# Removing DRAM row copies and following the array's current shape in a two-branch training step

## The chip, the cores and the metric

The kernel runs on one core of one Trainium2 chip. The time is the device time of one execution in microseconds (us), lower is better.

## The reference

The program computes a layer's output and all its gradients. The input `x` (2048 tokens of 512) is normalised to `xn`, and the output is `x + A(xn) + B(xn)`. All large arrays are bf16.

Branch A is attention with a memory that is carried along: the tokens are cut into 64 segments of 32, and each segment attends, with 32 heads of 128, to 8 memory rows and itself. The memory rows' own results are the memory of the next segment:

```python
mem = mem0
for s in range(n_seg):
    xs = x[:, s * seg_len:(s + 1) * seg_len, :].copy()
    h = jnp.concatenate([mem, xs], axis=1)
    q = jnp.einsum('btd,dhe->bhte', h, Wq)
    k = jnp.einsum('btd,dhe->bhte', h, Wk)
    v = jnp.einsum('btd,dhe->bhte', h, Wv)
    scores = jnp.einsum('bhqe,bhke->bhqk', q, k) * scale
    scores = jnp.where(mask[None, None], scores, -1000000000.0)
    p = _softmax(scores, axis=-1)
    o = jnp.einsum('bhqk,bhke->bhqe', p, v)
    o = jnp.einsum('bhte,hed->btd', o, Wo)
    mem = o[:, :M, :].copy()
    outs.append(o[:, M:, :])
```

Branch B is an MLP (512 to 1792 to 512) with a squared ReLU. `reference` returns the output and the gradients of `x`, `mem0`, the four attention weights and the MLP's weights and biases, by `jax.vjp`.

## The kernel before

The work goes in four stages. **First** the normalisation and the MLP, forward and backward, in 8 groups of 256 tokens (to about 245 us). It stores the MLP's activations and their gradients (`S_AT`, `S_GT1`). **Forward** come the 64 segments, one after the other, since each needs the memory of the one before: `chain(s)`. **Backward** the same 64 steps run from the last to the first. **Last** come the attention's weight gradients, 16 groups of long 128x128 products with 512 columns, at L1690 and L1694.

A block is four segments, 128 tokens. In the projections, a segment's 32 rows (8 memory rows in place of the first 8 tokens, and 24 tokens) are the narrow weights of 128x32 products: four such products lie side by side in the array, one for each group `j` of heads. The first 8 tokens of every segment need not wait in this chain: their projections do not depend on the memory, and their attention is not needed by the next segment. They are handled four segments at a time, off the chain: these are the "lead" rows of `l_proj`, `l_qkv`, `l_attn` (forward), `l_pre` and `l_post` (backward), whose tiles end in L (`ps_qL`, `ps_scL`, `ps_gL`).

TensorE's array thus takes three shapes, which the code calls by a letter: "f" is 128x128, "w" is 128x32 (four column groups), "d" is 32x32 on the diagonal. Projections, scores and memory products are "w", transposes (`to_T` at L546, `transpose_to` at L427) are "f", attention-weighted sums (`diag`) are "d".

Off-chain work fills the waits of the chain. In the forward stage these are the lead rows and the MLP's weight gradients, `dw_unit`: 14 units, each with 16 chunks of 128 tokens; a chunk is loaded into one of five buffers `sx` and enters two 128x128 products with 512 columns into `ps_dw` (L1254). Units 7 to 13 also transpose their result (`ps_wT`).

Nothing here runs in the order of the source. Every operation is handed to a planner, `_Plan` (L109), with its costs, its shape and what it reads and writes. `run` (L166) then fixes the order of all instructions of all engines: it ranks an operation by the longest path behind it, plus a hand-tuned number from the tables `BIAS`, and takes next what can start first. `PAR` has three constants for each stage: `grace`, added to the start of off-chain work, `idle`, how long an engine may be kept waiting for a better operation, and `keep`, a penalty on an operation whose shape differs from the array's. The planner counts 0.105 us for a change of shape (`_TURN`).

The results that the backward stage and the weight gradients need go through DRAM. Some are stored and then copied from DRAM to DRAM into another order of rows: `S_V` and `S_K` (keys and values of each segment), whose first 8 rows of each head group go on to `S_VM` and `S_KM`; the lead rows of `S_XN` and of the output gradient, to `S_HNL` and `S_GOL`; those of `S_B`, to `S_BL`; the lead rows of the output, which go to `S_OL` and from there to `out_0`. At a block's end, `blk_out` transposes all 128 rows of its input, memory rows included, back (`ps_hN`, backward `ps_gN`) and stores them to `S_HNA` and `S_GOA` by four DMAs. `HNc` and `GOc` are loaded from these for the weight gradients. All these DMAs but a few go through SyncE's queue (SP), in order.

Of the kernel before, what the change touches and what calls it, by code (L numbers as in the profile page):

```python
# [10 lines left out]
PAR = ((0.3, 0.3, 0.0), (0.61, 7.94, 4.04), (0.09, 2.05, 17.32))  # L11
BIAS_0 = None
BIAS_1 = {
    "l_proj": (
        47.2, 6.5, -41.1, 1.2, 0.8, -33.9, -14.2, 11.4, 20.3, -5.1, -5.3, -14.4, 17.4, 1.5, 7, 20.1, 4.7,
        25.3, -22.2, 55.6, -37, 19.3, -97.5, -1.4, 23, -6.1, -29.3, 48.8, 4.1, 4.5, 52.1, -159.3,
    ),
    "blk_in": (
        11.4, -35.6,
    ),  # L20
# [4 lines left out]
    ),  # L25
    "chain": (
# [4 lines left out]
    ),  # L31
    "blk_out": (
        16.8, -102.8, -36.2, -171.6, -10.2, -72.7, -50.6, -74.7, -96.5, 48.6,
    ),
    "l_attn": (
# [16 lines left out]
    ),  # L52
    "l_pre": (
        46.2, 1.1, -8.1, -100.3, 71, -115.1, -66.8, -4.6, 0.3, -83.5, 0.5, -9.3, -80.7, -12.7, -35.4, -15.9,
        26.3, 9.2, -131.2, 6, 10.9, -47, -9.6, -40.9, 6.9, -128.5, -6.9, -9.4, -61.5, 28.5, -31.2, -38.8,
        -146.2,
    ),
    "load": (
        -43.9, 14.3, -32.2, 2.7, 17.6, -33.7, -80.9, -102.8, 27.2, -48.1, 12.4, -79.8, 33.3, -39.3, -48,
        -45.5, -93.3, -170.2, -64.2, -40.6, -31.9, -8.7, -42, -6.3, 6.8, 15.9, 1.3, 13.8, -17.6, -62.2,  # L60
    ),
    "chain": (
# [5 lines left out]
    ),  # L68
    "blk_out": (
        -22.4, 26.1, -106.9, -65.1, -53.3, 31.4, -76.5,  # L70
    ),
    "l_post": (
# [3 lines left out]
    ),  # L76
# [12 lines left out]
_LINE = 128  # L89
_FETCH = 4.2  # L90


class _PE(dict):
    shape = None
    n = 8


def pe(cost, shape, n=8):
    x = _PE(PE=cost)
    x.shape = shape  # L100
    x.n = n
    return x
# [206 lines left out]
def kernel(  # L309
# [59 lines left out]
    JQ = 4  # L369
# [1373 lines left out]
```

## Time and profile before

| | |
|---|---|
| median of 3 runs | 2802.92 us (2802.28 to 2803.98) |
| span of the profiled execution, first to last instruction | 2798.3 us |
| mean granted TensorE clock | 0.995 |

The page gives no other time for the profiled execution than its span; the runs' median is 4.6 us longer than this span. TensorE's share of time is in two rows: PE is the products, PEld the loads of their weights, which overlap with them.

Rows of a timeline have the start, the length, engine, line and operation, then out<-in by the program's names, the array's shape (128\*32), the moving operand (128x512) and how many were merged. Products are pipelined: the next one starts well before the recorded end of the one before.

### The profile page before, as it was taken

The numbers are of one execution on the slowest core, as the hardware profiler recorded it, in microseconds if no ns is written. First come the engines' busy times: TensorE is split into PE (matmuls) and PEld (weight loads), VectorE is DVE, ScalarE is ACT, GpSimd is POOL, SyncE is SP. The second block draws the span as 40 slices with busy tenths as digits, with TensorE's granted clock in tenths as the row PEclk, the third lists the DMA queues.
The fourth block names the chain that finished last, engine by engine and source line by source line (L and its number), as shares of the span: only waits on it lengthen the run. The fifth ranks groups of instructions, "written<-read, shape, count | busy, mean of one in ns | idle before, by whom it ended". The sixth has DMA issues, their size and how long they took to land.

```text
span 2798.3 us, 125071 instructions
## 1 busy us (share of the span) xinstructions
PE 2664.6 (95%) x54888; PEld 1538.5 (55%) x55072; DVE 1327.3 (47%) x3327; ACT 985.8 (35%) x2012; POOL 824.8 (29%) x2431
## 2 busy tenths in 40 slices
PE   8998999999999999999999999999999899999999
PEld 6664555555555555575555555555555444444444
DVE  5544455555455555565455455555455402232322
ACT  4333444444444444364444444444444300000000
POOL 1111111111111111145555555555555301112210
PEclk9999999999999999999999999999999999999999
DMA  6657656555557566647777676777766698788861
GB/s 211 202 172 205 180 160 175 164 166 163 156 169 186 169 185 175 177 118 178 187 181 187 179 189 179 189 192 190 188 182 177 201 344 273 232 255 270 257 185 42
DMA packets 499792, 530.91 MB, mean 190 GB/s; under 512 B 223845, under 2 KB 325398, under 8 KB 497070
## 3 DMA queue, kind: packets, MB, share of 16 engines
q1 hardware_dynamic: 480254, 463.06, 59.9%
q0 software_dynamic: 15056, 53.56, 5.6%
q8 instruction: 430, 7.05, 1.1%
q10 hardware_dynamic: 3936, 6.29, 0.7%
q14 instruction: 116, 0.95, 0.1%
HBM read 249.77 MB, written 237.52 MB: 174 GB/s over the span
## 4 chain that ended last, share of the span: by engine, by line
PE 45%; DVE 4%; issue 3%; DMA 3%; ACT 1%; POOL 1%; SPq 0%; DVEq 0%; ACTq 0%; POOLq 0%
PE ps_gw L1690 14%; PE ps_dRA L1370 8%; PE ps_gw L1694 5%; PE ps_gO L538 3%; PE ps_dRL L1370 3%; PE ps_d L624 2%; DMA dLN<-S_GNL 2%; PE ps_d L573 1%; PE ps_d L599 1%; PE ps_gOT L429 1%; PE ps_d L588 1%; PE ps_gm L1524 1%; PE ps_gL L538 1%; PE ps_dL L1481 1%; PE ps_dP L1468 1%
## 5 line engine op out<-in xcount | busy, mean ns | idle before, releaser
L1370 PE MATMUL ps_dRA<-WA,dT 128*32 128x512 bf16 x6144 | 377.0, 381 | 5.3 <-issue 2.5
L1690 PE MATMUL ps_gw<-WA,WB 128*128 128x512 bf16 x1505 | 330.6, 379 | 1.6
L1690 PEld LDWEIGHTS <-WB 128*128 128x128 bf16 x1896 | 185.4, 98 | 225.0 <-issue 1.7
L538 PEld LDWEIGHTS <-PA 128*32 128x32 bf16 x8192 | 195.4, 96 | 192.3 <-DVE PA L1190 22.3
L435 ACT CAST dN<-ps_d 128x512 bf16<-128x512 f32 x372 | 207.4, 590 | 184.7 <-PE ps_d L599 112.3
L1370 PEld LDWEIGHTS <-dT 128*32 128x32 bf16 x6144 | 151.8, 96 | 154.2 <-DVE dT L517 17.3
L433 DVE CAST gwo<-ps_gw 128x512 bf16<-128x512 f32 x64 | 40.0, 685 | 399.9 <-PE ps_gw L1690 268.5
L435 ACT CAST gwo<-ps_gw 128x512 bf16<-128x512 f32 x64 | 33.1, 598 | 510.2 <-PE ps_gw L1690 357.3
L517 DVE STREAM_TRANSPOSE dT<-dN 128x256 f32<-128x256 f32 x384 | 165.4, 437 | 72.1 <-ACT dN L435 66.5
L1020 POOL TENSOR_TENSOR P<-P,rsA 128x320 bf16<-128x320 bf16 x64 | 46.2, 722 | 458.8 <-DVE rsA L1015 244.1
L624 PEld LDWEIGHTS <-PB 32*32 32x32 bf16 x8192 | 119.8, 92 | 76.4 <-DVE PB L1168 23.9
L1701 POOL DMA_DIRECT2D out_dram<-gwo x96 | 71.6, 753 | 293.9 <-ACT gwo L435 265.1
L538 PE MATMUL ps_q<-WA,PA 128*32 128x512 bf16 x2048 | 145.2, 382 | 5.5 <-DVE PA L1190 3.7
L1039 PE MATMUL ps_RA<-WB,OT 128*32 128x256 bf16 x4096 | 129.0, 277 | 17.7 <-DVE OT L517 13.6
L538 PE MATMUL ps_k<-WA,PA 128*32 128x512 bf16 x2048 | 144.9, 381 | 0.3 <-DVE PA L1190 0.3
L435 ACT CAST kN<-ps_k 128x512 bf16<-128x512 f32 x125 | 73.4, 587 | 194.1 <-PE ps_k L538 172.2
L538 PE MATMUL ps_v<-WA,PA 128*32 128x512 bf16 x2048 | 140.7, 379 | 0.0
L1039 PEld LDWEIGHTS <-OT 128*32 128x32 bf16 x4096 | 103.9, 98 | 46.2 <-DVE OT L517 32.0
L538 PE MATMUL ps_gO<-WB,PA 128*32 128x512 bf16 x2048 | 126.4, 380 | 1.0 <-DVE PA L1528 1.0
L611 POOL COPY BDL<-bPLL 32x64 bf16<-32x64 bf16 x256 | 60.4, 236 | 218.4 <-PE ps_d L573 210.4
L433 DVE CAST qN<-ps_q 128x512 bf16<-128x512 f32 x62 | 42.9, 692 | 171.5 <-PE ps_q L538 169.5
L1254 PE MATMUL ps_dw<-sx,anT 128*128 128x512 bf16 x339 | 108.2, 384 | 6.6 <-DMA sx<-S_XN 2.8
(315 smaller groups left out, 5300.8 us busy)
## 6 DMA issues: line engine op xcount, KB each, us to landing
S_GN<-dN SPq DMA_DIRECT2D x192, 256.0 KB
WA<-S_GN SPq DMA_DIRECT2D x150, 256.0 KB
S_Q<-qN SPq DMA_DIRECT2D x64, 256.0 KB
S_K<-kN SPq DMA_DIRECT2D x64, 256.0 KB
S_V<-vN SPq DMA_DIRECT2D x64, 256.0 KB
S_ON<-oN SPq DMA_DIRECT2D x64, 256.0 KB
bqN<-S_Q SPq DMA_DIRECT2D x64, 256.0 KB
bkN<-S_K SPq DMA_DIRECT2D x64, 256.0 KB
```

The costliest lines, as they stand in the source:

```text
L433: nc.vector.tensor_copy(out, in_)
L435: nc.scalar.copy(out, in_)
L517: self.plan.add({"DVE": 0.445}, lambda e, half=half: nc.vector.transpose(words(dst, half).rearrange("p (i c r) -> p i c r", i=4, c=2), src ...
L538: nc.tensor.matmul(bk()[32 * j:32 * (j + 1), :], lhsT=win(dc), rhs=Wt(dc, c0), start=(dc == 0), stop=(dc == DC - 1), tile_position=(0, 32 ...
L611: f(q_(dst, j)[:, :, j, 0:c], q_(src_f(), j))
L624: nc.tensor.matmul(bk()[32 * j:32 * j + m, k * P:(k + 1) * P], lhsT=lf(j, i), rhs=rf(j, i), start=(k == 0 and x == 0), stop=(x == n - 1), ...
L1039: nc.tensor.matmul(bk()[32 * c:32 * (c + 1), :], lhsT=sg.rows(OTt, i, j), rhs=Wo[:, JQ * i + j, dh * DH:(dh + 1) * DH], start=(i == 0 and ...
L1254: nc.tensor.matmul(bks[x]()[:], lhsT=anT[x][:, c, :], rhs=sx[z][:], start=(c == 0), stop=(c == TC - 1))
L1370: nc.tensor.matmul(bk()[32 * j:32 * (j + 1), :], lhsT=sg.rows(XT, i, j), rhs=wtf(t, i, j), start=(first and i == 0), stop=(last and i == N ...
L1690: nc.tensor.matmul(bks[n](), lhsT=HNc[:, rc, dc * P:(dc + 1) * P], rhs=gns[y][:, hf * 512:(hf + 1) * 512], start=(y == 0), stop=(y == NRC ...
L1694: nc.tensor.matmul(bks[n](), lhsT=gns[y][:, k * P:(k + 1) * P], rhs=GOc[:, rc, :], start=(y == 0), stop=(y == NRC - 1))
L1701: nc.gpsimd.dma_start(outWs[t][dc * P:(dc + 1) * P, 4 * hf:4 * hf + 4, j, :], wt[:].rearrange("p (i e) -> p i e", i=4))
```

## The change

**DRAM layouts.** `S_K`, `S_V`, `S_VL`, `S_ON`, `S_ONL`, `S_GN` and `S_GNL` get another order of dimensions, so that the memory rows of a block, or the rows of a weight gradient's chunk, can be read by one strided DMA. `S_VM`, `S_KM`, `S_HNA`, `S_HNL`, `S_GOA`, `S_GOL`, `S_BL` and `S_OL` go, with their copies. `blk_out` packs only the 8 memory rows of each segment (GpSimd), turns them by four 32-column products and stores them with one DMA to `S_HM` (backward `S_GM`). `HNc` and `GOc` are put together from `S_XN` (the output gradient for `GOc`) and these, by more and smaller loads. The rows of `VR` and `VTL` come in another order, so the GpSimd copies into `VT` read with a stride.

**Shapes.** An off-chain product can be given as "wf": the planner lets it run in the array's shape of the moment, "w" or "f", and changes the shape for it only if the array has neither. This holds for `ps_dw`, `ps_wT` and the lead rows' transposes (`ps_qLT`, `ps_kLT`, `ps_gLT`). As "w", a 128x128 product is four 128x32 products.

**Pairs.** `dw_unit` loads two chunks with one DMA, into three buffers of two chunks.

**Fewer products.** The lead scores `ps_scL` and their gradient `ps_dPL` take one product with 64 columns where there were two with 32. The chain's mask product covers 256 columns, not 320.

The planner's constants `PAR` of the forward and backward stages and all tables `BIAS` of these are new.

```diff
-PAR = ((0.3, 0.3, 0.0), (0.61, 7.94, 4.04), (0.09, 2.05, 17.32))
+PAR = ((0.3, 0.3, 0.0), (0.37, 216.29, 18.84), (0.09, 14.67, 24.36))
...
-                turn = o.shape not in (None, shape)
+                turn = bool(o.shape) and shape not in o.shape
...
-    S_K = dt_([NSEG, P, HW], BF16, "S_K")
-    S_V = dt_([NSEG, P, HW], BF16, "S_V")
+    S_K = dt_([TC, RA, JQ, SPB, HW], BF16, "S_K")
+    S_V = dt_([TC, RA, JQ, SPB, HW], BF16, "S_V")
...
+    def mixed_rows(t, c0, c1, base, mems):
+        ops = []
+        for v in range(SPB):
+            ops.append((t[RA * v + M:RA * (v + 1), c0:c1, :], base[c0 * P:c1 * P].rearrange("(c v r) d -> v r c d", v=SPB, r=RA)[v, M:]))
+        for v in range(SPB):
+            ops.append((t[RA * v:RA * v + M, c0:c1, :].rearrange("k c (y z) -> k (c y) z", y=DC),
+                        mems[c0:c1, :, M * v:M * (v + 1), :].rearrange("c y k z -> k (c y) z")))
+        return ops
...
     def transpose_to(ps_ap, in_ap, base=0, form="f"):
+        if form == "w":
+            for c in range(4):
+                x = slice(32 * c, 32 * c + 32)
+                nc.tensor.transpose(ps_ap[x], in_ap[:, x], ident[:], tile_position=(0, 32 * c))
+            return
...
         def to_T(self, kind, nm, src, skeys, out_f, okeys, prio):
+            form = "wf" if prio else "f"
...
-                    for c in range(2):
-                        for j in range(JQ):
-                            nc.tensor.matmul(q_(ps, j)[:, i, 32 * c:32 * c + 32], lhsT=qLT[p][:, i, j, :],
-                                             rhs=KT[p][:, :, i * JQ + j, M * c:M * c + M],
+                    for j in range(JQ):
+                        nc.tensor.matmul(q_(ps, j)[:, i, :].rearrange("p (c v k) -> p v c k", c=2, k=M), lhsT=qLT[p][:, i, j, :],
+                                         rhs=KT[p][:, :, i * JQ + j, 0:2 * M].rearrange("p v (c k) -> p v c k", c=2),
...
-                nc.tensor.matmul(q_(bs_(), j).rearrange("p i k -> p (i k)"), lhsT=ident[:, 32 * j:32 * (j + 1)],
-                                 rhs=maskA[:].rearrange("p i k -> p (i k)"), start=True, stop=False,
+                nc.tensor.matmul(q_(bs_(), j)[:, :, M:KA], lhsT=ident[:, 32 * j:32 * (j + 1)],
+                                 rhs=maskA[:, :, M:KA], start=True, stop=False,
...
-            for nm, D_, S_ in (("S_V", S_VM, S_V), ("S_K", S_KM, S_K)):
-                sg.dma(lambda D_=D_: mrow(D_[b])[:, M * v:M * (v + 1), :], lambda S_=S_: mrow(S_[s])[:, 0:M, :],
-                       [(nm, s)], [(nm + "M", b, v)])
...
-        sx = [tl("sx%d" % x, [P, D]) for x in range(5)]
+        sx = [tl("sx%d" % x, [P, 2, D]) for x in range(3)]
...
                 def mm(e, c=c, z=z):
+                    w = 32 if e == "w" else P
                     for x in range(2):
-                        nc.tensor.matmul(bks[x]()[:], lhsT=anT[x][:, c, :], rhs=sx[z][:], start=(c == 0), stop=(c == TC - 1))
-                A(pe(0.435, "f", 2), mm, [("sx", z), ("anT", 0, c // HC), ("anT", 1, c // HC)], [bks[0], bks[1]])
+                        for m in range(0, P, w):
+                            nc.tensor.matmul(bks[x]()[m:m + w, :], lhsT=anT[x][:, c, m:m + w], rhs=sx[z][:, c % 2, :], start=(c == 0),
+                                             stop=(c == TC - 1), tile_position=(0, m))
+                A(pe(0.435, "wf", 2), mm, [("sx", z), ("anT", 0, c // HC), ("anT", 1, c // HC)], [bks[0], bks[1]])
...
         def blk_out(b):
-            bk = sg.bank("f", [P, D], BF16, "ps_gN")
+            A({"POOL": 0.3}, lambda e: nc.gpsimd.tensor_copy(
+                gNat[:, 0:P].rearrange("p (c v k) -> p c v k", c=DC, k=M), gT[p].rearrange("p c (v r) -> p c v r", r=RA)[:, :, :, 0:M]),
+              [("gT", p)] + [("gm", p, v) for v in range(SPB)], ["gNat"])
+            bk = sg.bank("f", [P, P], F32, "ps_gN")
...
             def tr(e):
                 for dc in range(DC):
-                    transpose_to(bk()[:, dc * P:(dc + 1) * P], gT[p][:, dc, :])
+                    nc.tensor.matmul(bk()[32 * dc:32 * (dc + 1), :], lhsT=gNat[:, 32 * dc:32 * (dc + 1)], rhs=ident[:],
+                                     start=True, stop=True, tile_position=(0, 32 * dc), skip_group_check=True)
```

More of the change, by code (lines that the diff above doesn't have):

```diff
@@ L100, in pe @@
     x.shape = shape
-    x.n = n
+    x.n = {k: n * (4 if k == "w" and len(shape) > 1 else 1) for k in shape}
     return x
@@ L176, in run @@
         free, loose, used = {}, {}, {}
-        shape = None
+        shape = "-"
         line = count = 0
@@ L285, in run @@
                     elig.append(u)
-            seq.append((o, e))
+            seq.append((o, form if form and len(o.shape) > 1 else e))
         assert len(seq) == len(ops)
@@ L383 @@
     S_XN = dt_([S, D], BF16, "S_XN")
-    S_HNA = dt_([S, D], BF16, "S_HNA")
-    S_HNL = dt_([TC * RL, D], BF16, "S_HNL")
-    S_GOA = dt_([S, D], BF16, "S_GOA")
-    S_GOL = dt_([TC * RL, D], BF16, "S_GOL")
     S_B = dt_([S, D], BF16, "S_B")
-    S_OL = dt_([TC * RL, D], BF16, "S_OL")
-    S_BL = dt_([TC * RL, D], BF16, "S_BL")
     S_GXNB = dt_([S, D], F32, "S_GXNB")
@@ L472, in bank, with put @@
             return _Bank(self, kind, shape, dt, name, key)
-        def put(self, out_f, in_f, R, W, prio=1, lat=3.5, cost=0.5):
+        def put(self, out_f, in_f, R, W, prio=1, lat=3.5, cost=0.62):
             self.dma(out_f, in_f, R, W, prio, lat, cost, "POOL")
@@ L577, in blocks, with mixed @@
                            bk, lambda bk=bk: bk()[:], [(dst[0], half)], prio, EV_F)
-        def mixed(self, nm, pre, terms, rkeys, dst, prio, lift=0.0):
-            bks = [self.bank("d", [P, 512], F32, "ps_" + nm) for _ in range(2)]
-            for half in range(2):
+        def mixed(self, nm, pre, terms, rkeys, dst, prio, lift=0.0, full=False, inter=False, kind=None):
+            bks = [self.bank(kind or "d", [P, 512], F32, "ps_" + nm) for _ in range(2)]
+            for half in ((0, 1) if not inter else ()):
                 bk = bks[half]
@@ L592, in mixed, with mm0 @@
                 bk = bks[half]
+                if inter:
+                    def mm0(e, half=half, bk=bk):
+                        for k in range(4):
+                            for x, (lf, rf) in enumerate(pre):
+                                nc.tensor.matmul(bk()[:, k * P:(k + 1) * P], lhsT=lf(4 * half + k), rhs=rf(4 * half + k),
+                                                 start=(k == 0 and x == 0), stop=False, skip_group_check=True)
+                    self.plan.add(pe(0.22 * len(pre), "f", 4 * len(pre)), mm0, rkeys[0](half), [bk], prio, lift=lift)
                 def mm(e, half=half, bk=bk):
@@ L1600, in mm0 @@
                                      start=(y == 0), stop=False)
[L1601 removed]
+            A(pe(0.86, "f", 4), mm0, [("gn", y), *[("HN", 0, n) for n in range(2 * SPB)], "gNat"], pw0)
         plan.run()
@@ L1673 @@
                 if x == 2 * JQ:
-                    for S_, r0, r1 in ((S_GOA, 0, TC), (S_GOL, TC, NRC)):
-                        dma(GOc[:, r0:r1, :], S_.rearrange("(c p) d -> p c d", p=P))
+                    for o_, i_ in (*mixed_rows(GOc, 0, TC, gflat, S_GM), *[lead_rows(GOc, n, gflat) for n in range(NLC)]):
+                        dma(o_, i_)
                 lns = [ln_in(b) for b in LNQ.get(x, [])]
```

245 lines of the change are left out of this document (128 added, 117 removed), and 51 rows, old and new, of tables (BIAS_1, BIAS_2).

## Prediction

> **What bounds the kernel now.** I read the page first, then the busy time by stretch, then TensorE's timeline inside one step, then the waits.
>
> ```profile
> span 2798.3 us, 125071 instructions
> PE 2664.6 (95%) x54888; PEld 1538.5 (55%) x55072; DVE 1327.3 (47%) x3327; ACT 985.8 (35%) x2012; POOL 824.8 (29%) x2431
> ```
>
> TensorE is busy for 2664.6 of 2798.3 us and no other engine comes near half of that. So a change is worth what it takes off TensorE, wherever TensorE is what a step waits for. The stretches tell where that is (columns: length, then busy time and count of PE, PEld, DVE, ACT, POOL, the clock, DMA share, GB/s):
>
> ```profile
> 249.30:1188.60 939.30, 881.53 (x22667) 525.22 (x22776) 497.71 (x1215) 412.01 (x857) 131.67 (x242) 0.99 0.61 172
> 616.40:631.50 15.10, 14.80 (x399) 9.25 (x403) 7.97 (x20) 6.50 (x15) 2.36 (x5) 1.00 0.50 170
> 631.50:645.50 14.00, 11.30 (x309) 6.76 (x304) 6.98 (x17) 7.29 (x17) 2.13 (x4) 1.00 0.52 146
> 1303.10:2208.50 905.40, 870.90 (x24562) 518.84 (x24561) 471.68 (x1175) 375.40 (x747) 502.68 (x1784) 1.00 0.71 184
> 2238.00:2798.00 560.00, 551.98 (x2549) 250.86 (x2593) 147.50 (x242) 33.73 (x65) 93.84 (x137) 1.00 0.74 232
> ```
>
> The first row holds 62 forward steps (from the memory product of step 0 to that of step 62), 15.15 us each. Rows two and three are two of them. In one TensorE is busy for 14.80 of 15.10 us: it is the limit. In the other for 11.30 of 14.00: that step waits for the recurrence itself. So the chain allows about 14.0 us, and the average lies 1.1 us above. The fourth row is most of the backward steps, the fifth the weight gradients at the end, where TensorE runs at 99% and nothing in the change alters its work. What "busy" hides is the array's change of shape. One forward step:
>
> ```profile
> 1000.34 1.04 PE L538 MATMUL ps_qL<-WA,PB 128*32 128x512 bf16 x16
> 1001.31 0.40 PE L429 MATMUL ps_qLT<-ident,lN 128*128 128x128 bf16 x4
> 1001.54 0.39 PE L429 MATMUL ps_wT<-ident,wt 128*128 128x128 bf16 x4
> 1001.76 0.59 PE L1254 MATMUL ps_dw<-sx,anT 128*128 128x512 bf16 x2
> 1002.29 0.23 PE L624 MATMUL ps_o<-vN,PB 32*32 32x128 bf16 x4
> ...
> 1003.29 0.39 PE L1254 MATMUL ps_dw<-sx,anT 128*128 128x512 bf16 x1
> ...
> 1004.48 1.93 PE L1039 MATMUL ps_RA<-WB,OT 128*32 128x256 bf16 x64
> 1006.35 1.04 PE L1254 MATMUL ps_dw<-sx,anT 128*128 128x512 bf16 x3
> 1007.47 0.22 PE L1185 MATMUL ps_mem<-sel,PB 128*32 128x16 bf16 x8
> 1007.62 0.60 PE L1254 MATMUL ps_dw<-sx,anT 128*128 128x512 bf16 x2
> 1008.15 0.62 PE L538 MATMUL ps_q<-WA,PA 128*32 128x512 bf16 x8
> 1008.59 1.04 PE L538 MATMUL ps_k<-WA,PA 128*32 128x512 bf16 x16
> 1009.46 0.60 PE L538 MATMUL ps_q<-WA,PA 128*32 128x512 bf16 x8
> 1009.89 0.60 PE L538 MATMUL ps_k<-WA,PA 128*32 128x512 bf16 x8
> ...
> 1011.62 0.31 PE L1153 MATMUL ps_sc<-maskA,ident 128*32 128x320 bf16 x4
> 1011.86 0.40 PE L429 MATMUL ps_qT<-ident,qN 128*128 128x128 bf16 x4
> ...
> 1014.37 0.39 PE L1102 MATMUL ps_scL<-maskL,ident 128*32 128x512 bf16 x4
> 1014.59 0.67 PE L1108 MATMUL ps_scL<-KT,qLT 128*32 128x32 bf16 x64
> 1015.08 0.62 PE L538 MATMUL ps_v<-WA,PA 128*32 128x512 bf16 x8
> ```
>
> Read starts, not durations, since the products are pipelined. Sixteen 128x32 products followed by the same shape take 0.87 us (1008.59 to 1009.46). The same sixteen followed by a 128x128 transpose take 0.97 (1000.34 to 1001.31). A change of shape thus costs 0.10 us. Two 128x128 gradient products plus a change take 0.53 (1007.62 to 1008.15), where eight 128x32 products, the same columns, take 0.43 (1009.46 to 1009.89): again 0.10, and the narrow shape loses nothing. From 1000.34 to 1015.08 there are ten changes (one of them, from ps_kT back to ps_v, in the last rows left out). Four belong to the chain, which must go to 32x32 for ps_o and to 128x128 for ps_qT. The other six exist only because ps_dw, ps_qLT and ps_wT insist on 128x128.
>
> **Term 1, shapes.** Counted off the whole timeline, the forward stretch has 531 changes and the backward one 548. Runs of 128x128 products that hold nothing but ps_dw, ps_qLT, ps_kLT, ps_wT, ps_hN (forward) and ps_gLT, ps_gN (backward) number 169 and 39. The first and last of each:
>
> ```profile
> 257.78 0.40 PE L429 MATMUL ps_qLT<-ident,lN 128*128 128x128 bf16 x4
> 1180.72 0.82 PE L1254 MATMUL ps_dw<-sx,anT 128*128 128x512 bf16 x2
> 1357.87 0.40 PE L429 MATMUL ps_gN<-ident,PA 128*128 128x128 bf16 x4
> 2168.25 0.40 PE L429 MATMUL ps_gN<-ident,PA 128*128 128x128 bf16 x4
> ```
>
> The change lets exactly these run as 128x32. A run between two 128x32 neighbours then saves two changes, one beside a 32x32 run saves one. Forward: 74 of the first kind, 88 of the second, 7 between two 32x32 runs that save none: 236 changes. Backward: 38 of the first kind: 76. At 0.096 us (the 0.10 above, as most changes of the timeline repeat it) that is 22.7 + 7.3 = 30.0 us of TensorE time. If the planner still takes a change here and there, less; the bounds are 0 and, with all beyond the four of each forward step gone, (531 - 248) x 0.096 = 27 forward.
>
> The Trainium skill, "TensorEngine Tiling (Array Packing)", Key Properties, says that changing the tiling mode drains TensorE, and the trace agrees in kind. "TensorE: Matmul & The Clock Gate", Step-by-step, puts the drain at about 128 cycles, an estimate of 53 ns at 2.4 GHz; by that the term would be 17 us. No sum here uses it, since the rows show 0.10 us.
>
> **Term 2, products dropped.** Each block's two full transposes (ps_hN, ps_gN: four products, 0.22 us by 1001.54 to 1001.76) become four 32-column products. Their price is that of four such products side by side:
>
> ```profile
> 2196.19 0.23 PE L1481 MATMUL ps_dL<-gON,BPK 128*32 128x128 bf16 x4
> 2196.24 0.23 PE L1481 MATMUL ps_dL<-gLN,BLK 128*32 128x128 bf16 x4
> ```
>
> 0.055 us, so 0.165 x 32 = 5.3 us. The 64 lead scores ps_scL take 0.49 (1014.59 to 1015.08); as 32 of twice the width they have the columns of the four mask products, 0.22 (1014.37 to 1014.59): 0.27 x 16 = 4.3, or nothing if the strided operands slow them. The lead gradient scores (L1404) change alike, another 4.3 or nothing. The mask takes 0.24 with a change, 0.14 without; 256 instead of 320 columns save 0.03 x 64 = 1.8. Together 15.7, at least 7.
>
> **Term 3, copies.** The copies S_VM, S_KM, S_HNL, S_GOL, S_BL, S_OL go, the four 32 KB stores of each block and direction become one, and the gradient's loads halve in number. They lie on the SyncE queue, which is in order, so a copy that waits for its source holds what is behind it.
>
> ```profile
> L624 PE MATMUL ps_oL<-VM,PTLL 32*32 32x128 bf16 x480 | 16.2, 214 | 2.0 <-DMA VM<-S_VM 2.0
> SPq L479 <- DMA S_K<-kN: 43.3, 22, 4.5
> ```
>
> SyncE stands 43.3 us for stores to land, yet TensorE lost only 2.0 us to a copy. I take 2. Before the weight gradients, five loads of HN become twenty smaller ones. I cost them at nothing, because the last chain steps and l_post(0) run meanwhile; uncovered, each us by which one lands late would count. Added: 32 small GpSimd copies beside an engine busy for 29% of the span, and some 1,800 more forward products (448 gradient products and 312 transposes times three, less 512 scores). Both are hidden if the instruction stream keeps up, below. GpSimd's VT copies now read with a stride; GpSimd is busy for 503 of 905 us in the backward stretch, so even half as long again is covered.
>
> **The sum.** 30.0 + 15.7 + 2 = 48 us off TensorE. Where TensorE is the limit it counts in full, where the chain is the limit not at all. I take two thirds forward (22.7 + 2.6 + 4.3 + 1.8 + 2 = 33, so 22), as the two steps shown stand for both kinds and the average is nearer the upper, and half backward (7.3 + 2.7 + 4.3 = 14, so 7), where TensorE is already at 96%. That is 29: 2798 becomes 2769 in the profile. The median of the runs lies 4.6 us above the profiled span, so 2774.
>
> **Rivals.** The order of all instructions comes from a planner whose constants and tables are new throughout, so the size of the capture is the main doubt.
>
> *Fillers fit the gaps* (chance 0.2). Work that costs no change can be put into any wait of the chain. Forward steps then come down from 15.15 to about 14.4 us, near the 14.0 shown: 62 x 0.75 = 46, with backward 14: 60, so 2742. For it: the gaps are there. Against: many end on VectorE results, too short to fill.
>
> *The chain swallows it* (0.14). TensorE waits longer where it now changes shape. A fifth is captured, 10 us: 2793. Against it speaks the 14.80 of 15.10.
>
> *The chain queues behind fillers* (0.1). The penalty on an operation that changes shape rises from 4.04 to 18.84 forward and 17.32 to 24.36 backward, and what still changes shape is the chain. If its two entries per forward step each wait behind one 0.43 us group, that costs 2 x 0.43 x 62 = 53 us. It decides once 29 / 0.43 = 67 of the 124 entries wait; with all of them, 2774 + 53 = 2827. Against it: the same penalty also keeps groups together.
>
> *Instruction supply* (0.04). 1,800 more on 22,667 forward products is 8%, or 26.7 per us at 917 us; the backward stretch keeps up 24562 in 905 us, 27.1 per us. So it decides only in bursts. If the queue gave no more than that rate and all 1,800 came on top at its 0.037 us, 66 us would be added: 2840.
>
> *Narrow weight loads* (0.02). If the four loads of a narrow product no longer hid behind products, 448 x 0.29 = 129 us would come on top (4 x 96 ns against 98):
>
> ```profile
> L1690 PEld LDWEIGHTS <-WB 128*128 128x128 bf16 x1896 | 185.4, 98 | 225.0 <-issue 1.7
> L1370 PEld LDWEIGHTS <-dT 128*32 128x32 bf16 x6144 | 151.8, 96 | 154.2 <-DVE dT L517 17.3
> ```
>
> That gives some 2900. The 0.43 us for eight narrow products, loads included, speaks against it. The Trainium skill states the rule behind it in "TensorEngine Tiling (Array Packing)", Restrictions: column tiling disables Fast Weight Load; the trace shows no cost of that here.
>
> **How the numbers follow.** The forecast, 2774 (own range 2760 to 2791, captures of nine tenths to a quarter), has 0.5. The range runs from 2742, the full filling of gaps, to 2806, where the queueing rival has taken all of the gain: it leaves out half of the first and most of the last three. This measurement can tell 0.2% (5.6 us) from nothing. Faster by more: the forecast, the fillers, and most of the swallowing: 0.82. Within: 0.04. Slower: 0.14.
>
> **What would show it.** Right: forward changes of shape near 300 and backward near 470, ps_dw in 128*32 groups of eight at 0.43 us, the forward stretch about 22 us shorter, the backward one 7, the weight gradients unchanged. Wrong: changes gone but as much TensorE waiting in their place (swallowed); ps_qT and ps_o starting later after VectorE has delivered (queued); more idle time before TensorE put down to "issue" (supply).

## The result, and the profile after

The changed kernel takes 3291.89 us (median of 4 runs, 3280.2 to 3293.75) where the kernel before takes 2803.45 (2802.28 to 2807.08): 1.173 times as long, 95% interval 1.171 to 1.175. The forecast was 29 us less; it came out 488 us more, far outside the range. From the page after, the rows on the totals and on the DMAs:

```profile
span 3289.6 us, 127787 instructions
PE 2774.8 (84%) x56460; PEld 1614.0 (49%) x56460; DVE 1331.0 (40%) x3315; ACT 998.8 (30%) x2042; POOL 845.4 (26%) x2460
GB/s 208 209 170 159 134 127 143 145 141 150 143 134 146 143 134 115 99 112 145 143 138 139 137 141 142 138 137 140 139 138 138 130 133 280 288 226 228 303 231 42
DMA packets 491022, 517.41 MB, mean 157 GB/s; under 512 B 221793, under 2 KB 317298, under 8 KB 488930
```

The same two DMA rows of the page before:

```profile
GB/s 211 202 172 205 180 160 175 164 166 163 156 169 186 169 185 175 177 118 178 187 181 187 179 189 179 189 192 190 188 182 177 201 344 273 232 255 270 257 185 42
DMA packets 499792, 530.91 MB, mean 190 GB/s; under 512 B 223845, under 2 KB 325398, under 8 KB 497070
```

TensorE's share falls from 95% to 84%: it now waits for more of the time. Fewer bytes move (517 MB for 531), but in the two stages of 64 steps they move at some 140 GB/s where it was 160 to 190. In the last sixth of the row, the weight gradients, the rate is what it was. By stretch (columns as in the prediction), cut where it cut, with its fifth row's stretch last:

```profile
257.50:1344.90 1087.40, 915.72 (x24268) 571.21 (x24264) 466.46 (x1167) 439.61 (x923) 136.46 (x258) 0.95 0.65 137
1417.20:2679.00 1261.80, 983.92 (x25720) 574.04 (x25721) 533.46 (x1281) 376.36 (x740) 545.00 (x1888) 0.91 0.69 137
2729.00:3289.60 560.60, 556.81 (x2627) 251.81 (x2619) 147.97 (x243) 33.83 (x65) 93.57 (x137) 1.00 0.78 232
```

The backward row runs from the first to the last memory-gradient product (`ps_gm`); before, that stretch is this:

```profile
1259.20:2209.00 949.80, 912.01 (x25805) 543.76 (x25807) 495.46 (x1234) 394.41 (x784) 528.17 (x1873) 1.00 0.72 184
```

So 148 us are lost in the forward steps (939.3 to 1087.4), 312 in the backward ones, and the DMA engines are as busy as before (0.65 for 0.61; 0.69 for 0.72) while they move a fifth or a quarter less in the time. TensorE's granted clock falls too, from 0.99 and 1.00 to 0.95 and 0.91, so some of its products run slower. What the engines wait for is data from DRAM. Five groups of the waits after (engine, line, what it waited for: total us, times, longest), three of TensorE in the forward stretch, then one of TensorE and one of VectorE in the backward one, where TensorE waits for VectorE and VectorE for a load:

```profile
PE ps_oL L654 <- DMA VM<-S_V: 39.1, 14, 6.5
PE ps_dw L1280 <- DMA sx<-S_XN: 24.3, 10, 3.6
PE ps_dw L1280 <- DMA sx<-in_grad_out_dram: 23.5, 9, 3.8
PE ps_dP L1492 <- DVE gOT L432: 132.1, 26, 11.4
DVE LT L534 <- DMA dLN<-S_GNL: 215.4, 28, 14.0
```

The last was this before:

```profile
DVE LT L517 <- DMA dLN<-S_GNL: 34.3, 21, 2.9
```

`sx`, now two chunks for each load, still comes in rows of 1 KB from arrays whose layout nobody touched. So it is not only the transfers with a new layout that have become slower. The pairs are not the reason: in e8 below, which keeps them and takes the layouts back, no wait of TensorE for `sx` is listed.

For all kernels that ran, this is the length of each stage in us, cut at the first and last `ps_mem` and `ps_gm` product of each profiled execution (the whole table is worked out from the timelines). Ratios are against runs of the kernel before from the same session, whose median was 2793.66 to 2803.45 us. Two kernels with the same shapes and all but the same order (e8 and e12) differ by 10 us in the forward stage, so a single stage is trusted to about that.

| kernel | first | forward | between | backward | end |
|---|---|---|---|---|---|
| before | 249.3 | 939.3 | 70.6 | 949.8 | 589.3 |
| after | 257.5 | 1087.4 | 72.3 | 1261.8 | 610.5 |
| e1 before, new K and V layout | 251.3 | 1133.5 | 74.6 | 980.4 | 589.1 |
| e2 before, V at 8 KB pitch | 250.0 | 937.4 | 71.3 | 945.0 | 590.7 |
| e3 after, old K and V layout | 261.4 | 1003.4 | 72.8 | 1190.0 | 608.6 |
| e4 after, old V layout | 261.3 | 1023.9 | 70.2 | 1253.2 | 610.0 |
| e5 after, transfers split | 261.4 | 971.8 | 69.8 | 1123.9 | 604.0 |
| e6 before, Q and output 4 x 32 rows | 249.1 | 1125.9 | 71.1 | 978.2 | 591.3 |
| e7 as e1, transfers split | 250.6 | 998.1 | 71.6 | 964.4 | 589.4 |
| e8 after, all layouts repaired | 262.0 | 936.4 | 71.0 | 948.7 | 597.8 |
| e9 as e6, 8 x 16 rows | 249.8 | 976.8 | 70.7 | 957.1 | 816.7 |
| e10 as e6, 16 x 8 rows | 249.8 | 953.5 | 71.1 | 950.4 | 645.8 |
| e11 as e8, products 128x128 only | 257.6 | 953.0 | 70.7 | 952.0 | 597.4 |
| e12 as e8, one load later | 256.4 | 946.9 | 69.7 | 952.1 | 597.0 |
| e13 before, shape choice alone | 250.9 | 940.3 | 72.8 | 954.7 | 590.0 |

### The profile page after: what moved, and what is told of

Same layout as the page of the kernel before. It is cut to its first block, busy times and chain, and to the rows that moved or that the text cites. A ratio compares the mean times of both kernels' runs of the same rounds, so it can differ in the third digit from the quotient of the medians.

```text
span 3289.6 us, 127787 instructions
## 1 busy us (share of the span) xinstructions
PE 2774.8 (84%) x56460; PEld 1614.0 (49%) x56460; DVE 1331.0 (40%) x3315; ACT 998.8 (30%) x2042; POOL 845.4 (26%) x2460
## 4 chain that ended last, share of the span: by engine, by line
PE 60%; DMA 26%; issue 6%; DVE 4%; SPq 2%; ACT 1%; POOL 0%; DVEq 0%; ACTq 0%; POOLq 0%
PE ps_gw L1721 12%; DMA dLN<-S_GNL 8%; PE ps_dRA L1395 7%; DMA bqN<-S_Q 5%; PE ps_gw L1725 4%; PE ps_v L555 3%; PE ps_h L827 3%; PE ps_k L555 3%; DMA VM<-S_V 3%; PE ps_dRL L1395 3%; PE ps_q L555 2%; PE ps_d L654 2%; PE ps_RA L1069 2%; DMA sx<-in_grad_out_dram 2%; DMA S_V<-vN 2%
## 5 line engine op out<-in xcount | busy, mean ns | idle before, releaser
L1395 PE MATMUL ps_dRA<-WA,dT 128*32 128x512 bf16 x6144 | 410.8, 408 | 40.7 <-issue 25.0
L555 PEld LDWEIGHTS <-PA 128*32 128x32 bf16 x8192 | 229.6, 100 | 222.3 <-issue 49.0
L1395 PEld LDWEIGHTS <-dT 128*32 128x32 bf16 x6144 | 162.3, 102 | 219.2 <-issue 76.3
L432 DVE COPY KT<-ps_kT 128x512 bf16<-128x512 bf16 x128 | 48.7, 419 | 327.3 <-PE ps_kT L428 327.3
L1280 PE MATMUL ps_dw<-sx,anT 128*32 128x512 bf16 x1792 | 123.2, 390 | 48.1 <-DMA sx<-S_XN 24.3
L555 PE MATMUL ps_k<-WA,PA 128*32 128x512 bf16 x2048 | 159.1, 404 | 3.5 <-DVE PA L1217 1.8
L555 PE MATMUL ps_q<-WA,PA 128*32 128x512 bf16 x2048 | 155.9, 397 | 0.9 <-issue 0.9
L641 POOL COPY BDP<-bP 32x256 bf16<-32x256 bf16 x256 | 100.8, 394 | 198.3 <-PE ps_d L591 192.1
L1492 PE MATMUL ps_dP<-bVT,gOT 128*32 128x40 bf16 x2048 | 36.4, 188 | 132.3 <-DVE gOT L432 132.1
L534 DVE STREAM_TRANSPOSE LT<-dLN 128x256 f32<-128x256 f32 x96 | 40.4, 425 | 232.7 <-DMA dLN<-S_GNL 218.6
```

The source lines that it names most:

```text
L432: nc.vector.tensor_copy(out, in_)
L534: self.plan.add({"DVE": 0.445}, lambda e, half=half: nc.vector.transpose(words(dst, half).rearrange("p (i c r) -> p i c r", i=4, c=2), src ...
L555: nc.tensor.matmul(bk()[32 * j:32 * (j + 1), :], lhsT=win(dc), rhs=Wt(dc, c0), start=(dc == 0), stop=(dc == DC - 1), tile_position=(0, 32 ...
L641: f(q_(dst, j)[:, :, j, 0:c], q_(src_f(), j))
L1280: nc.tensor.matmul(bks[x]()[m:m + w, :], lhsT=anT[x][:, c, m:m + w], rhs=sx[z][:, c % 2, :], start=(c == 0), stop=(c == TC - 1), tile_posi ...
L1395: nc.tensor.matmul(bk()[32 * j:32 * (j + 1), :], lhsT=sg.rows(XT, i, j), rhs=wtf(t, i, j), start=(first and i == 0), stop=(last and i == N ...
```

## The experiments

The theories. **E**, engines: in the new layouts the 128 rows of a 256 KB transfer are no longer one dimension of equal stride, but 4 head groups by 32 rows. Such a transfer would go over 4 of the 16 DMA engines only, and whatever else has a share on these four would wait behind it. **L**, layout: the rows lie further apart (32 KB for 2 KB or 8 KB), and this is slow by itself, for the transposing load of V (L1) or for every access (L2). **O**, order: the planner's new order is the bad one.

**e1: one layout alone.** Before, with the new order of dimensions for K and V; the order of all work is kept.

```diff
-    S_K = dt_([NSEG, P, HW], BF16, "S_K")
-    S_V = dt_([NSEG, P, HW], BF16, "S_V")
+    S_K = dt_([TC, RA, JQ, SPB, HW], BF16, "S_K")
+    S_V = dt_([TC, RA, JQ, SPB, HW], BF16, "S_V")
...
-            sg.dma(lambda: S_V[s], lambda: flat(vN), ...
+            sg.dma(lambda: step_rows(S_V, s), lambda: flat(vN), ...
```

> The kernel before with one thing of the change: S_K and S_V in the new order of dimensions, so that the rows of a step are written and read at a pitch of 8 and 32 KB; the copies S_VM and S_KM stay, and the order of all operations stays. Theory L (the layout): rows at such a pitch make the DMAs slow, the queue backs up and TensorE waits. Then this kernel is slower than 2803 us by hundreds of us, about 3000 to 3300. Theory O (the new order of operations starts things too early for their data): no difference, 2795 to 2815.

3035.85 us, ratio 1.083 (1.080 to 1.086). Two 256 KB stores per step cost 194 us of forward stage, in the old order: O is not needed for the loss.

**e2: the pitch of V alone.** Before, with V at 8 KB from row to row, its 128 rows still one dimension.

```diff
-    S_V = dt_([NSEG, P, HW], BF16, "S_V")
+    S_V = dt_([TC, P, SPB, HW], BF16, "S_V")
```

> The kernel before with only S_V at a pitch of 8 KB between rows, as S_Q has it already. The store of a step then looks like that of S_Q; what is new is that the transposing load into VR reads rows at this pitch. Theory L1 (the transposing load of spaced rows is the slow one): the backward stage alone gets slower, by 100 to 300 us, so 2900 to 3100. Theory L2 (only the wider pitch of 32 KB hurts, in stores and plain loads): within 15 us of 2803. Theory O: 2803.

2801.63 us, ratio 0.9996 (0.998 to 1.001). A pitch of 8 KB costs nothing, the transposing load of it included. That rules out L1 at this pitch; 32 KB comes with e7.

**e3 and e4: the layouts taken back in the changed kernel**, for K and V, and for V alone (their memory rows are then gathered as before, or by four DMAs in place of one).

```diff
-    S_K = dt_([TC, RA, JQ, SPB, HW], BF16, "S_K")
-    S_V = dt_([TC, RA, JQ, SPB, HW], BF16, "S_V")
+    S_K = dt_([NSEG, P, HW], BF16, "S_K")
+    S_V = dt_([NSEG, P, HW], BF16, "S_V")
```

> The changed kernel with S_K and S_V stored step by step without gaps, as before; the memory rows are loaded by four DMAs instead of one, and VM is stored once per block for the backward stage. The order of operations is the changed one. Theory L: the loss goes, 2750 to 2800 us. Theory O: the loss stays, 3200 to 3300.

> The changed kernel with S_V alone stored without gaps, S_K in the new layout. Theory L1 (the transposing load): nearly all of the loss goes, under 2850 us. Theory L2 (the pitch of 32 KB in plain stores and loads): about half goes, 2950 to 3100, as keys and values move the same bytes. Theory O: 3200 to 3300.

3134.26 us, ratio 1.118 (1.115 to 1.122), and 3220.93, 1.149 (1.147 to 1.152). e3 met no range, e4 that of O. About a third of the loss goes with K and V, 84 us forward and 72 backward. The output and the three gradients, whose stores are of the same kind, are still in the new layout, and the backward stage still has 240 us too much.

**e5: the transfers split.** The changed kernel; each such transfer becomes four of 64 KB, one per head group, whose rows are one dimension of 32.

```diff
+    def split_j(q, out, in_):
+        for j in range(JQ):
+            q.dma_start(out(j), in_(j))
...
-                sg.dma(lambda: S_GN[t, b][:, v], lambda: flat(dN[t]), both("dN%d" % t), [])
+                A({"SP": T_DMA}, lambda e: split_j(nc.sync, lambda j: S_GN[t, b][j, v], lambda j: q_(flat(dN[t]), j)), both("dN%d" % t), [], 1, 3.2)
```

> The changed kernel with the same DRAM layouts and the same order, but each of its 256 KB transfers whose outermost dimension is the 4 head groups (the stores of K, V, the output and the three gradients, and the load of K) is issued as four transfers of 64 KB, one for each head group, whose outermost dimension is the 32 rows. Theory E (a transfer is spread over as many DMA engines as divide its outermost dimension, here 4 of 16, and these four then hold up everything else): the loss of 488 us mostly goes, 2770 to 2850 us, forward step near 15.3 us, with 9 to 12 more issues in SP's queue per step as what is left. Theory L (the wide row pitch of the layouts is slow by itself) and theory O (the order in which the planner now puts the work is the bad one): both are kept here, so the time stays at 3250 to 3300 us.

3031.12 us, ratio 1.085 (1.083 to 1.087): half of the loss comes back, far less than E said. The forward stage is down to 971.8, the backward one still at 1123.9. There SyncE issues 25.8 DMAs per step, where the changed kernel has 13.8 and the one before 14.5, and is occupied by issuing for 84% of the stage, where they have 66% and 58% (counted off its timeline). The fuller queue may be a new limit, so this run does not measure the engines alone.

**e7: e1 again, split in the same way.**

```diff
-            sg.dma(lambda: step_rows(S_V, s), lambda: flat(vN), ...
+            A({"SP": T_DMA}, lambda e: split_j(nc.sync, lambda j: S_V[b][:, j, v], lambda j: q_(flat(vN), j)), ...
```

> The first experiment again (the kernel before with the new layout of K and V), with its stores and the load of K issued as four transfers of 64 KB by head group. The 32 KB pitch is kept, the outermost dimension is 32. Theory E: 2800 to 2840 us, nearly all of the 233 us come back. Theory L (32 KB pitch): stays near 3035 us.

2877.47 us, ratio 1.030 (1.028 to 1.032), between the two ranges. e1 lost 233 us against the kernel before, this one 84. With the 32 KB pitch kept, two thirds come back, so L2 is not the cause of these. The 84 us that stay go with a SyncE queue that is 81% occupied in the forward stage (63% before); that the queue causes them is argued, not shown, and a part for the pitch of 32 KB is not ruled out.

**e6, e9 and e10: the engines counted out.** Before, with spare rows in the arrays of Q and of the output. Nothing else about their stores changes: the pitch stays 8 KB, the order stays, the bytes stay. One spare row after each 32 makes the 128 rows 4 x 32, one after each 16 makes them 8 x 16, one after each 8, 16 x 8.

```diff
-    S_Q = dt_([TC, P, SPB, HW], BF16, "S_Q")
+    S_Q = dt_([TC, JQ, RA + 1, SPB, HW], BF16, "S_Q")     # e9: [TC, 8, 17, ...], e10: [TC, 16, 9, ...]
...
-    S_ON = dt_([TC, P, SPB, HW], BF16, "S_ON")
+    S_ON = dt_([TC, JQ, RA + 1, SPB, HW], BF16, "S_ON")   # likewise
```

> The kernel before with one thing changed: the DRAM arrays of Q and of the output have one spare row after each 32 rows, so that the row pitch stays 8 KB and the order of all work stays, but the 128 rows of a transfer can no longer be one dimension and its outermost is 4. Theory E: the forward pass loses about what the same trick on K and V cost in the first experiment (two 256 KB stores a stage over 4 engines; 233 us there), and the backward pass a little by the load of Q: 2950 to 3060 us. Theory L and theory O: pitch and order are those of before, so 2795 to 2810 us.

> As the kernel with a spare row after each 32 rows of Q and the output (3011 us), but with a spare row after each 16 rows, so that the outermost dimension of the two stores is 8. Theory E (as many DMA engines as divide the outermost dimension): half the engines, so the loss of 217 us shrinks to well under half, 2800 to 2900 us. A rival (N) that any pattern of two row dimensions is slow by itself, however many engines: 3000 us or more.

> The same with a spare row after each 8 rows, so that the outermost dimension is 16. The pattern is as broken up as before (more so), but all 16 engines divide it. Theory E: 2790 to 2810 us, nothing lost. Rival N: 3000 us or more.

3010.91 us, ratio 1.077 (1.074 to 1.081); 3067.92, 1.094 (1.090 to 1.098); 2873.40, 1.025 (1.021 to 1.028). The totals of e9 and e10 missed what E expected, and that of e9 lies where the rival N put it. But look at the stages. Forward stretch of e6, of e9, of e10:

```profile
249.10:1375.00 1125.90, 943.40 (x22776) 548.54 (x22776) 500.25 (x1215) 410.14 (x857) 132.81 (x242) 0.94 0.66 143
```

```profile
249.80:1226.60 976.80, 891.80 (x22667) 530.96 (x22776) 497.89 (x1215) 411.38 (x857) 131.35 (x242) 0.98 0.65 165
```

```profile
249.80:1203.30 953.50, 885.87 (x22675) 528.18 (x22784) 498.13 (x1215) 412.05 (x857) 131.41 (x242) 0.99 0.63 169
```

With 4, 8 and 16 as the outermost dimension the stage loses 187, 38 and 14 us, and the one load per backward step 28, 7 and 1. A pattern of two row dimensions is not slow in itself, so N is out; one with few pieces outermost is. The traces allow the engines to be counted: in them a DMA of SyncE's queue leaves packets of 4 bytes, 15.1 in the mean in the kernel before, so about one for each of the 16 engines. In the forward stretch this queue has 253.5 per step before, 228.9 in e6, 237.1 in e9, 253.0 in e10, that is 24.6, 16.4 and 0.5 fewer. Two stores that go from 16 engines to 4, 8 and 16 would leave 24, 16 and 0 fewer. How long SyncE stands at a transposing load, which is unchanged in all of them (min/median/max in ns; before, e6, e9, e10), follows:

```profile
L1244 SPq DMA_TRANSPOSE anT<-S_GT x28: 1231/1326/2642, 766.7 to 1158.8; - x28
```

```profile
L1249 SPq DMA_TRANSPOSE anT<-S_GT x28: 1337/2157/5412, 870.3 to 1341.9; - x28
```

```profile
L1249 SPq DMA_TRANSPOSE anT<-S_GT x28: 1232/1554/3468, 785.8 to 1196.1; - x28
```

```profile
L1249 SPq DMA_TRANSPOSE anT<-S_GT x28: 1237/1400/2442, 771.9 to 1172.4; - x28
```

Where then are the 227 us of e9 and the 57 us of e10 at the end? In a second use of the output that the expectation had overlooked. The weight gradients read it 32 rows of each segment at a time. With gaps after 16 rows this read is 2 x 16 rows, with gaps after 8 rows 4 x 8, and with gaps after 32 it is whole. SyncE's timeline, issuing these 256 KB loads: before, e9 and e10 (start, length, line, count):

```profile
2630.79 15.93 SPq L1660 DMA_DIRECT2D WA<-S_ON  x14
```

```profile
2822.69 66.19 SPq L1665 DMA_DIRECT2D WA<-S_ON  x14
```

```profile
2707.50 32.84 SPq L1665 DMA_DIRECT2D WA<-S_ON  x14
```

1.14, 4.73 and 2.35 us for one. And while nothing but these loads runs in e9, the stretches are (last two columns DMA share and GB/s):

```profile
2870.00:2880.00 10.00, 0.00 (x0) 0.00 (x0) 0.00 (x0) 0.30 (x1) 0.00 (x0) 0.75 0.13 50
2880.00:2887.00 7.00, 0.00 (x0) 0.00 (x0) 0.00 (x0) 0.00 (x0) 0.00 (x0) 0.50 0.13 50
```

A share of 0.13 is 2 of 16 engines, and they move 50 GB/s, 25 each. TensorE has no work at all meanwhile. This settles theory E: the count of engines follows the outermost dimension (2, 4, 8, 16), and the loss follows the count. That the other transfers lose by waiting on the same engines is the likely reading, not a measured one: no view lists transfers by engine.

The Trainium skill states this rule in "DMA: Bandwidth & Descriptors", section "Why a DMA increments its semaphore by 16 and not by 1": a transfer uses the largest number of engines, at most 16, that divides the slowest dimension of both its sides. The trace agrees: 24.6, 16.4 and 0.5 fewer packets where that rule gives 24, 16 and 0. The same page's Specifications give about 27 GiB/s for one engine, which is 29 GB/s; the trace shows 25 GB/s, and the measurement decides.

**e8: the changed kernel repaired.** Its new order, its shape choice and its pairs are kept. K, V, the output and the gradients lie as before, the memory rows of V are copied once per block again, and the rows of `HNc` and `GOc` are put together in the order that this needs. `S_VL`, `S_ONL` and `S_GNL` keep the new order.

```diff
-    S_ON = dt_([TC, JQ, SPB, RA, HW], BF16, "S_ON")
-    S_GN = dt_([3, TC, JQ, SPB, RA, HW], BF16, "S_GN")
+    S_ON = dt_([TC, P, SPB, HW], BF16, "S_ON")
+    S_GN = dt_([3, TC, P, SPB, HW], BF16, "S_GN")
...
-            ops.append((t[RA * v + M:RA * (v + 1), c0:c1, :], ...
+            ops.append((t[SPB * M + v:P:SPB, c0:c1, :], ...
```

> The changed kernel with its new order of products and its paired gradient tokens, but with the layouts of before for K and V (one gapless block per stage), for the output and for the gradients (row, then stage), so that each 256 KB transfer has 128 rows as its outermost dimension; the memory rows of V go through the extra copy of before again, and the memory loads are four transfers. Theory E: 2740 to 2800 us, at or below the kernel before, since the 30 us of saved array-shape changes are then all that differs. Theory O (the new order is bad by itself): above 3000 us. If only a part of the loss is by the engines: between.

2815.83 us, ratio 1.007 (1.005 to 1.009), where it was 1.173: nearly all of the loss was the layouts of these four. It is still above the range of E, 2740 to 2800. Its forward and backward stretches:

```profile
262.00:1198.40 936.40, 869.26 (x24272) 547.52 (x24264) 465.11 (x1166) 437.58 (x923) 135.77 (x257) 1.00 0.58 163
1269.40:2218.10 948.70, 904.48 (x25723) 542.21 (x25726) 527.18 (x1281) 371.53 (x740) 537.13 (x1888) 1.00 0.68 182
```

They are as long as before (-3 and -1 us), not shorter. What is left lies before the first step (12.7 us) and behind the last (8.5 us). In these two places TensorE has waits that it meets once:

```profile
PE ps_vL L557 <- POOL PB L1093: 12.1, 1, 12.1
```

```profile
PE ps_dRA L1400 <- DVE dT L536: 9.5, 2, 9.3
PE ps_gN L1577 <- POOL maskL L1570: 7.4, 1, 7.4
```

The two waits behind the last step lead back to the change. For the first, this is what holds ScalarE, before and in e8:

```profile
2216.35 1.07 ACT L435 CAST dN<-ps_d 128x512 bf16<-128x512 f32 x2 [3.82 <-DMA WB<-S_GN]
2230.87 1.07 ACT L435 CAST dN<-ps_d 128x512 bf16<-128x512 f32 x2 [9.64 <-DMA WB<-S_GN]
```

ScalarE issues some of the loads for the weight gradients itself. Before, these were 8 in 4.3 us, two of them for `HNc`; in e8 they are 14 in 10.1 us, eight of them for `HNc`, and the conversion of `dN`, for which VectorE and then TensorE wait, comes behind them. The second is GpSimd's new packing of the memory rows:

```profile
2250.51 0.29 POOL L1570 COPY maskL<-PA 128x128 bf16<-128x128 bf16 x1 [15.21 <-DMA out_dram<-maskL]
```

It writes the buffer from which the memory's gradient is still to be stored, and that store stands in SyncE's queue among loads of `HNc`. The same two waits are in e11 (9.3 and 6.4 us) and e12 (9.3 and 7.7). No run took them away, so their price is read from the traces alone.

**e11: what the shapes are worth in the new order.** As e8, but the choice is always 128x128; order and all else are kept.

```diff
-                o.fn(e)
+                o.fn("f" if o.shape and len(o.shape) > 1 else e)
```

> The changed kernel with the repaired layouts (2816 us), with each operation in the same place, but the off-chain products always as 128x128 and never as 128x32. By the repaired kernel's trace this brings back 270 changes of the array's shape in the forward steps, 56 in the backward steps and 8 outside, 334 x 0.095 us = 31.7 us at face value. The prediction's step (two thirds of the forward changes and half of the backward ones come out of the time): +20 us, ratio 1.0135 to 1.0145. The rival that the chain swallows them (the steps wait for their own results anyway): under +8 us, ratio 1.006 to 1.010.

2832.63 us, ratio 1.011 (1.009 to 1.013), between the two ranges. By the ratios that is 11 us above e8, whose interval it just touches, and 15 above e12 (next), which ran beside it and has the shapes of e8. Counted off the timelines, e11 has 326 more changes than e8 (334 were expected). They are worth about a third to a half of their face value here, less than the prediction's step and more than the rival, but the intervals leave room for nearly nothing and for most of it.

**e12: one load later.** As e8, with the first transposing load of `anT` taken out of SyncE's queue ahead of the first step and put before the next one.

```diff
+        late = [n for n, x in enumerate(seq) if x[0].cost == {"SP": 1.7}]
+        if late:
+            x = seq.pop(late[0])
+            seq.insert(late[1] - 1, x)
```

> The changed kernel with the repaired layouts, with one transposing load (the first half of the first gradient token pair) taken out of its place in SP's queue ahead of the first step and put just before the next such load, some 22 us later. If this load is what makes the first step wait 12.1 us for its mask, by the 5 us that it holds SP's queue and by what it pushes back: 5 to 12 us faster than the repaired kernel, ratio 1.002 to 1.005. If the wait has another cause: unchanged, ratio 1.0065 to 1.007.

2819.36 us, ratio 1.005 (1.003 to 1.007), not told apart from e8. The wait at `ps_vL` is 5.5 us here, but 8.5 in e11 and 12.1 in e8. These two both have the load in its place and differ by more than e11 and e12 do, so what makes the wait is open.

**e13: the shape choice alone, in the old order.** Before, with each group's form picked after the planning: 128x32 behind 128x32 work.

```diff
+            if getattr(o.cost, "flex", False):
+                nxt = next((x.shape or "f" for x in on_pe[n:] if not getattr(x.cost, "flex", False)), "f")
+                now = "w" if now == "w" or (now == "d" and nxt == "w") else "f"
+                forms[o.idx] = now
```

> The kernel before with the shape choice alone: its layouts, its loads and its order of work stay, and only at the end each group of the weight gradient's products and each off-chain transpose that stands behind 128x32 work is issued as 128x32. By the trace of before this takes 223 changes of shape out of the forward steps and 52 out of the backward steps, 275 x 0.095 us = 26.1 us at face value. The prediction's step (two thirds in the forward, half in the backward pass): 223 x 0.095 x 2/3 + 52 x 0.095 / 2 = 16.6 us faster, ratio 0.993 to 0.995. The rival that the chain swallows them: under 5 us, ratio 0.998 to 1.001. A rival that the narrow products cost something of their own (four weight loads of 32 columns for one of 128): slower, above 1.002.

2810.74 us, ratio 1.003 (1.002 to 1.004): slightly slower. Counted off its timeline, the changes of shape fall from 532 to 309 forward and from 580 to 528 backward, as they should. Yet the forward stretch is as long as before:

```profile
250.90:1191.20 940.30, 884.00 (x24868) 542.70 (x24872) 498.04 (x1215) 410.71 (x857) 131.30 (x242) 0.99 0.61 172
```

21 us of changes are gone and nothing is gained. (TensorE's busy time, 884.00 for 881.53, can't be compared to some us: in the stretch before, 109 of 22776 products have left no record.) The total, 1.003, is what the rival of costly narrow products said, but its rows speak against it. Sixteen narrow gradient products followed by narrow work take 0.86 us, 0.43 for eight, what two wide ones took in the prediction's rows (0.53 with a change of 0.10):

```profile
759.20 1.04 PE L1271 MATMUL ps_dw<-sx,anT 128*32 128x512 bf16 x16
760.06 1.92 PE L1054 MATMUL ps_RA<-WB,OT 128*32 128x256 bf16 x64
```

With the same products at the same price, 21 us less of changes and the same length, TensorE must wait some 22 us more (an estimate, the 21 and the 1 us by which the stretch is longer). In this order the step's length, 15.17 us for 15.15, is then not set by TensorE's changes of shape but by the results that the next step waits for: the chain swallows them. Where the 8 us of the total come from is open; the backward stretch has 5 of them, less than a stage varies by.

## Why the prediction was wrong, step by step

**The step that failed is Term 3.** It priced what the copies cost and gained, and the layouts that replace them at nothing: no row of the prediction asks how the new patterns of `S_K`, `S_V`, `S_ON` and `S_GN` are spread over the DMA engines. They are the loss: without them the ratio falls from 1.173 to 1.007 (e8). What to ask stood in the change itself, whose diff takes `S_K` and `S_V` from 128 rows in one dimension to 4 head groups by 32 rows. None of the rivals was this one; the slow ones put the danger into TensorE's queue, its weight loads and its instruction stream. Where the prediction read waits on DMAs (2.0 us of TensorE, 43.3 us of SyncE), it read them for the buffer that they hold, never for what else is on the same engines. The same term put the many small loads of `HNc` at nothing; in e8's trace ScalarE's issuing of them holds its next conversion for 9.64 us where it was 3.82, a good part of the 8.5 us lost behind the last step.

**The capture.** 22 us forward and 7 backward were taken from the spare time between 15.15 us and a "chain" of 14.0. In the old order the shape choice alone gives nothing (e13), in the new one some 11 to 15 us for all stages (e11 against e8 and e12), and e8's two stretches are no shorter than before. So the rival "the chain swallows it", 0.14, was the truer account of that part, though not of the time; the row with 14.80 of 15.10 us busy was read as proof of a TensorE limit, but e13 takes 0.3 us of changes out of each step and the step stays. A busy TensorE in one profile does not say that the step would end earlier with less work.

**What held.** The counts of the changes of shape: forward 532 to 295, backward 580 to 484, so 237 and 96 fewer (said: 236 and 76; "near 470" was counted from 548 on the shorter backward stretch). The narrow shape of the gradient products shows no cost: all run as 128x32 after the change, and e8, which has them so, is faster than e11, which has none. So the rival of narrow weight loads is out, and so is the instruction supply in e8, where forward has 24272 products in 936 us. That the weight gradients are unchanged: 556.81 of 560.60 us busy at 232 GB/s. The chain queueing behind fillers is not seen in e8, whose forward steps are as long as before. One reading was off without harm: VectorE's 1327.3 us are half of TensorE's 2664.6.

**What stays open.** What makes the wait before the first step in the repaired kernel; with those behind the last it is about the 0.7% by which that kernel lies above the one before. And what of e5's and e7's rest is SyncE's queue. Term 2 was not measured alone. No version here beats the kernel before.

## What to carry to other kernels

Before a DRAM array is laid out anew, write down the outermost dimension of every transfer that touches it, on both sides, second uses included: it should be a multiple of 16, or the transfer runs on fewer engines (here with 2, 4 and 8) and other transfers slow down with it. The sign in a profile is a DMA share that stays while GB/s falls, and unchanged loads that take longer. And time taken off an engine that is busy for 98% of a step counts only after a run without that work has shown the step to be shorter.

## What the runs showed of the hardware

A store of 256 KB in 4 pieces of 32 rows, twice per step of 15 us, slowed transposing loads that share nothing with it from 1.33 to 2.16 us in the median (e6). The packets themselves took longer: in the forward stretch those of 256 bytes 54 ns in the mean for 28 before, those of 2 KB 119 for 91. Sixteen pieces of 8 rows still cost the forward stage 14 us more than one dimension of 128, little above the 10 us by which e8 and e12 differ in this stage.

TensorE's clock falls in an idle stretch and comes back late. In e8's timeline, after the wait of 12.1 us, eight narrow products take nearly twice as long as eight of the same kind before it:

```profile
237.31 0.60 PE L557 MATMUL ps_vL<-WA,PB 128*32 128x512 bf16 x8
250.05 1.04 PE L557 MATMUL ps_vL<-WA,PB 128*32 128x512 bf16 x8 [12.14 <-POOL PB L1093]
...
251.73 1.07 PE L557 MATMUL ps_vL<-WA,PB 128*32 128x512 bf16 x8
...
255.89 0.61 PE L557 MATMUL ps_qL<-WA,PB 128*32 128x512 bf16 x8
```

The granted clock is 0.66 in the wait itself (238 to 250 us), 0.50 in the 4 us behind it, 0.64 in the next two and 1.00 after 256. So TensorE runs at half rate for some 5.4 us, and the wait of 12 us costs some 2.7 us more behind it (an estimate, half of these). The granted clock of e9's idle stretches above, 0.75 and then 0.50, shows the same fall. The Trainium skill, "TensorE: Matmul & The Clock Gate", Part 1, describes this gate, at half rate when TensorE has not been busy; the 0.50 agrees.
